# Three key tiles of 128 and a block diagonal rest tile in a fused attention and feed-forward kernel

## The chip, the cores and the metric

The kernel runs on one core of a Trainium2 chip. The metric is the device time of one execution in microseconds (us), the median of several runs; lower is better. Most runs of one kernel agree within about 1%. A profile of one execution comes with each kernel. Engines are named as the profile names them: PE (TensorE matmul), PEld (TensorE weight load), DVE (VectorE), ACT (ScalarE), POOL (GpSimd) and SP (SyncE, which issues most DMAs here; SPq is its queue).

## The reference, cut to what matters

There are 8 batches of 12 heads, 448 tokens and a head size of 64. The heads are worked in pairs, so there are 6 pairs per batch and 48 in all. After the attention comes a feed-forward layer of 768 by 2048 by 768.

```python
q_n = q / sqrt(mean(q*q, -1) + 1e-6) * g_q          # k_n likewise
scores = (1 / sqrt(64)) * q_n @ k_n.T
attn = softmax(scores)
x = (attn @ v)  -> [3584, 768]
h = x @ w_in
out = (h * clip(h + 3, 0, 6) / 6) @ w_out
```

Everything arrives in 32-bit floats; the kernel multiplies in bf16.

## The kernel before

The program is a list of steps. Each step names the engine or engines that may take it, an estimate of its time, and the steps that it must wait for. A greedy planner in the kernel's own source orders the steps of each engine once, before the program is built, so on the chip every engine runs a fixed order. "Batch 2's slot" is the stretch in which the attention of batch 2 runs; the feed-forward work of batch 1 runs in the same stretch.

Loads: three DMAs per pair, each of 112 partitions with four tokens of each head (1024 contiguous bytes).

```python
def heads(src, P):
    b, j = divmod(P, NJ)
    return src[b, 2*j:2*j+2, :, :].rearrange("h (p t) d -> p h (t d)", t=T)      # T = 4
def loads(P):
    for i, src in enumerate((k, q)):
        e = "ACT" if i and P < 3 else "SP"
        add(e, 0.47, at - 26, lambda: dma_start(out=qk[0:PT, i], in_=heads(src, P)), ...)   # PT = 112
    add("SP", 0.47, at - 19, lambda: nc.sync.dma_start(out=vf[0:PT], in_=heads(v, P)), ...)
```

Preparation: squares, their sums on VectorE, the norm factor on ScalarE, then one scaling of k and one of q, on VectorE or GpSimd (GpSimd alone from batch 2 on).

```python
red = add("DVE", 0.6 * n, ..., tensor_reduce(out=ssq, in_=sq ...))
r   = add("ACT", 0.45, ..., rstd, red)
sc.append(add({"DVE": 0.69, "POOL": 1.05}, 0, ..., tensor_tensor(qks, qk, rs4 (broadcast), MULT), r, lock=True))
```

Then come the transposes of k and q (on PE for the first ten pairs, by DMA after), four score steps of 112 keys per pair (two matmuls each, one per head, on the two halves of the PE's rows), one exp of 896 columns per step, and 64 value matmuls of 65 columns per two pairs.

## Time and profile before

The median is 442.9 us (441.35 to 443.99). The first table of the profile gives the busy time of each engine, its share of the span and the number of its instructions:

```profile
PE 410.6 (94%) x3663; PEld 229.2 (52%) x3682; DVE 246.3 (56%) x417; ACT 249.0 (57%) x425; POOL 240.2 (55%) x230
```

The windows table gives the busy time of each engine per stretch, with the number of instructions in brackets. After the engines come the granted TensorE clock (1.00 is full), the busy share of the core's DMA engines and the rate they moved, in GB/s. The kernel before:

```profile
core 0: us, PE busy (x) PEld busy (x) DVE busy (x) ACT busy (x) POOL busy (x), PEclk, DMA share, GB/s
0.00:10.00 10.00, 0.00 (x0) 0.00 (x0) 0.44 (x1) 2.39 (x4) 3.34 (x18) 1.00 0.88 241
10.00:20.00 10.00, 4.62 (x28) 1.89 (x29) 9.85 (x14) 7.01 (x17) 4.52 (x6) 1.00 1.12 249
20.00:30.00 10.00, 9.52 (x120) 6.23 (x121) 9.07 (x17) 8.59 (x13) 8.29 (x9) 1.00 1.15 266
30.00:40.00 10.00, 8.78 (x136) 5.63 (x132) 8.91 (x20) 8.73 (x15) 9.55 (x10) 1.00 1.18 254
40.00:90.00 50.00, 45.63 (x485) 26.34 (x486) 38.08 (x65) 35.49 (x65) 44.45 (x43) 1.00 1.06 209
90.00:140.00 50.00, 49.41 (x452) 26.06 (x453) 33.62 (x52) 32.80 (x56) 31.68 (x28) 1.00 0.63 163
```

PE is nearly full from 60 us on. In 10 to 40 us VectorE is 89 to 98% busy, GpSimd fills up too, and the DMA share is over 1. The chain of waits that ended last puts most of the span on PE:

```profile
PE 80%; POOL 5%; DVE 4%; ACT 3%; issue 3%; DMA 3%; SPq 1%; POOLq 0%
```

The timeline of SP in 20 to 31 us (start, duration in us, source line, what is loaded from what) shows how long the issue of one load holds the queue, here mostly 0.31 us:

```profile
24.08 0.31 SPq L302 DMA_DIRECT2D qk<-in_q_dram  x1
24.64 0.31 SPq L306 DMA_DIRECT2D vf<-in_v_dram  x1
27.90 0.31 SPq L302 DMA_DIRECT2D qk<-in_k_dram  x1
```

The list of DMA issues gives count, size and median time from issue to landing over the whole run:

```profile
qk<-in_k_dram SPq DMA_DIRECT2D x48, 224.0 KB, 3.3
vf<-in_v_dram SPq DMA_DIRECT2D x48, 224.0 KB, 3.7
```

### The profile page before, as it was taken

Reading aid. Unit: us, or ns where it says so; the run is one execution under the profiler, and the core shown is the slowest. Engines: PE = TensorE matmul, PEld = TensorE weight load, DVE = VectorE, ACT = ScalarE, POOL = GpSimd, SP = SyncE. Lnnn points to the kernel's source line nnn. Section 1 sums busy time; section 2 is a strip of 40 time slices with the busy share of each in tenths; the row PEclk is TensorE's granted clock in tenths of the full one; section 3 lists DMA queues with packets and bytes.
Section 4 is the critical chain, followed back from the end, with each engine's and each line's share of the span. In section 5 each row is a group of like instructions: output and inputs, shape, how many; then the busy total and the mean of one; then the engine's idle time right before and its main releaser. Section 6 shows DMA issues by size and latency. Waiting matters only on the chain.

```text
span 438.6 us, 9205 instructions
## 1 busy us (share of the span) xinstructions
PE 410.6 (94%) x3663; PEld 229.2 (52%) x3682; DVE 246.3 (56%) x417; ACT 249.0 (57%) x425; POOL 240.2 (55%) x230
## 2 busy tenths in 40 slices
PE   0588799999999999999999999999999999999995
PEld 0355455555455565554455565554455555654563
DVE  1998887657674564456555465556564444334421
ACT  3788588657765666367664677357673665123200
POOL 3499988855757567656765657747757510000000
PEclk9999999999999999999999999999999999999999
DMA  8999999877545745674465655684465420220122
GB/s 241 247 265 261 224 214 193 216 197 192 128 121 148 189 113 136 167 214 111 133 156 157 177 135 145 159 214 109 120 161 164 97 56 12 54 81 0 37 72 73
DMA packets 102923, 64.58 MB, mean 147 GB/s; under 512 B 59744, under 2 KB 99424, under 8 KB 102880
## 3 DMA queue, kind: packets, MB, share of 16 engines
q1 hardware_dynamic: 94544, 57.01, 50.6%
q0 software_dynamic: 7296, 6.29, 9.1%
q10 hardware_dynamic: 1040, 0.69, 0.5%
q8 instruction: 29, 0.48, 0.5%
q14 instruction: 14, 0.11, 0.1%
HBM read 45.61 MB, written 11.01 MB: 129 GB/s over the span
## 4 chain that ended last, share of the span: by engine, by line
PE 80%; POOL 5%; DVE 4%; ACT 3%; issue 3%; DMA 3%; SPq 1%; POOLq 0%
PE M L558 27%; PE M L533 25%; PE S L416 9%; PE X L437 8%; PE S L558 4%; PE R L437 2%; PE S L533 2%; DVE ssq L337 1%; ACT e L421 1%; POOL qks L351 1%; PE X L558 1%; POOL sq L322 1%; POOL va L359 1%; DMA gq_t<-in_g_q_dram 1%; POOL sq L329 1%
## 5 line engine op out<-in xcount | busy, mean ns | idle before, releaser
L421 ACT ACTIVATE e<-S 112x896 bf16<-112x896 f32 x192 | 166.3, 914 | 64.1 <-PE S L416 64.0
L533 PE MATMUL M<-xT,w_in_sb 128*128 128x384 bf16 (+1 forms) x679 | 145.1, 349 | 3.7 <-DVE gT L541 2.9
L351 POOL TENSOR_TENSOR qks<-qk,rs 112x512 bf16<-112x512 f32 x87 | 90.5, 1055 | 86.6 <-ACT rs L344 84.7
L558 PE MATMUL M<-w_out_sb,gT 128*128 128x384 bf16 x736 | 131.8, 326 | 0.0
L558 PEld LDWEIGHTS <-gT 128*128 128x128 bf16 x896 | 82.9, 98 | 57.8 <-issue 7.8
L533 PEld LDWEIGHTS <-w_in_sb 128*128 128x128 bf16 x768 | 69.6, 97 | 67.4 <-issue 12.5
L541 DVE SCALAR_TENSOR_TENSOR gT<-t,M 128x384 bf16<-128x384 f32 (+1 forms) x116 | 70.6, 611 | 59.1 <-ACT t L539 58.3
L539 ACT ACTIVATE t<-M 128x384 f32<-128x384 f32 (+1 forms) x116 | 62.6, 540 | 67.0 <-PE M L533 65.5
L437 PEld LDWEIGHTS <-e 112*128 112x128 bf16 x1536 | 65.1, 99 | 31.4 <-issue 16.0
L337 DVE TENSOR_REDUCE ssq<-sq 112x16 f32<-112x1024 f32 (+1 forms) x49 | 58.4, 1193 | 23.3 <-POOL sq L329 12.2
L329 POOL TENSOR_TENSOR sq<-qk 112x1024 f32<-112x1024 f32 x36 | 68.1, 1892 | 0.0
L416 PE MATMUL S<-kq,kp 64*128 64x448 bf16 x384 | 56.6, 364 | 4.1 <-DVE kp L381 1.7
L437 PE MATMUL X<-va,e 112*128 112x65 bf16 x1152 | 58.6, 196 | 0.8 <-ACT e L421 0.6
L566 DVE COPY y<-M 128x384 f32<-128x384 f32 x46 | 25.6, 556 | 59.2 <-PE M L558 59.0
L359 POOL CAST va<-vf 112x512 bf16<-112x512 f32 x48 | 31.5, 658 | 10.4 <-DMA vf<-in_v_dram 10.1
L392 POOL TENSOR_SCALAR kp<-kq,gp 128x448 bf16<-128x448 bf16 x23 | 32.3, 1402 | 5.3 <-DMA kq<-qks 5.2
L463 DVE TENSOR_TENSOR xn<-X,rd 128x384 bf16<-128x384 f32 x48 | 26.8, 558 | 1.6
L416 PEld LDWEIGHTS <-kp 64*128 64x128 bf16 x384 | 12.2, 94 | 27.7 <-issue 18.0
L437 PE MATMUL R<-va,e 112*128 112x65 bf16 x384 | 20.4, 195 | 0.0
L377 PE MATMUL M<-ident,qks 112*128 112x112 bf16 x80 | 7.9, 242 | 13.0 <-DVE qks L351 12.4
L558 PE MATMUL S<-w_out_sb,gT 128*128 128x384 bf16 x112 | 19.5, 326 | 0.0
L462 DVE RECIPROCAL rd<-X 128x6 f32<-128x6 f32 x48 | 9.2, 192 | 15.3 <-PE X L437 15.2
(42 smaller groups left out, 156.2 us busy)
## 6 DMA issues: line engine op xcount, KB each, us to landing
qk<-in_k_dram SPq DMA_DIRECT2D x48, 224.0 KB, 3.3
vf<-in_v_dram SPq DMA_DIRECT2D x48, 224.0 KB, 3.7
qk<-in_q_dram SPq DMA_DIRECT2D x45, 224.0 KB, 3.4
w_in_sb<-in_moe_w_in_dram POOLq DMA_DIRECT2D x4, 768.0 KB, 11.3
w_out_sb<-in_moe_w_out_dram POOLq DMA_DIRECT2D x4, 768.0 KB, 11.9
out_dram<-y SPq DMA_DIRECT2D x8, 336.0 KB, 3.1
out_dram<-y SPq DMA_DIRECT2D x8, 288.0 KB, 3.4
out_dram<-y SPq DMA_DIRECT2D x8, 240.0 KB, 3.2
```

Source lines behind the costliest of these rows:

```text
L329: parts = [add("POOL", 1.93, at - 10, lambda: nc.gpsimd.tensor_tensor(out=sq[0:PT], in0=qk[0:PT], in1=qk[0:PT], op=MULT), *ld, *war, lock= ...
L337: red = add("DVE", 0.6 * n, at - 8 * hurry + 0.5 * i0, lambda i0=i0, i1=i1, cs=cs: nc.vector.tensor_reduce(out=ssq[0:PT, cs], in_=sq[0:PT, ...
L351: sc.append(add(on, 0, at - 6 * hurry, lambda e, i=i, rs4=rs4: engines[e].tensor_tensor(out=qks[0:PT, i].rearrange("p t h d -> p h t d"), ...
L359: vc = add({"POOL": 0.61}, 0, at - 3, lambda e: engines[e].tensor_copy(out=va[0:PT, :, :, 0:D], in_=vf[0:PT].rearrange("p h (t d) -> p h t ...
L392: nc.vector if e == "DVE" else nc.gpsimd).tensor_scalar_mul(
L416: nc.tensor.matmul(out=ps[:, a, 0:S], lhsT=kp[rows, c0:c0 + 128], rhs=kq[rows, 1, :], start=True, stop=True)
L421: x = add("ACT", 0.93, at + step * (t0 + i) / T + 0.2, lambda t=t0 + i, ps=ps: nc.scalar.activation(out=e[0:PT, t], in_=ps[0:PT, :, 0:S], ...
L437: nc.tensor.matmul(out=dst[:, a * E1:(a + 1) * E1], lhsT=e[0:PT, t, a, c0:c0 + 128], rhs=va[0:PT, a, t, :], start=(first and a == 0 and t ...
L533: nc.tensor.matmul(out=m[:, 0:n], lhsT=w_in_sb[:, kt, f * 128:(f + 1) * 128], rhs=X[:, kt, :], start=(kt == 0), stop=(kt == NKT - 1))
L539: r = add("ACT", 0.08 + n / 1200, due + span, lambda: nc.scalar.activation(out=t[:, 0:n], in_=m[:, 0:n], func=RELU, bias=0.5, scale=1.0 / ...
L541: g = add("DVE", 0.12 + n / 960, due + span, lambda: nc.vector.scalar_tensor_tensor(out=G[:, f, :], in0=t[:, 0:n], scalar=1.0, in1=m[:, 0: ...
L558: nc.tensor.matmul(out=m[:, 0:HALF], lhsT=G[:, f, i * 128:(i + 1) * 128], rhs=w_out_sb[:, f, cols], start=(f == 0), stop=(f == NFT - 1))
```

## The change

The intent is to take work off PE. 448 keys are cut into three tiles of 128 and a rest of 64 instead of four tiles of 112. The rests of the two heads of a pair share one tile, laid out block diagonally: the rows of head 0 carry head 0's rest keys in columns 0 to 63, those of head 1 in columns 64 to 127. Two pairs then need seven score steps instead of eight, and 48 full value matmuls and 16 half-row ones instead of 64. The price is a load of k and of v in two DMAs each, and one more VectorE instruction per pair, which scales the rest keys and sets them on the diagonal by a mask. Besides, only 8 instead of 10 pairs are transposed on PE, no feed-forward output group of batch 0 stays in its own slot (two groups, 5.2 us of PE, move one slot later), and the small loads of g go to the front of ScalarE's queue, pair 0's q to SP's. From batch 1 on the pairs are worked two at a time, and the results of the value matmuls go to one PSUM tile (X) instead of two (X and R).

```diff
+    def load_tiled(e, at, tile_, src, P, war, cost, after):
+        x = heads(src, P)                                        # [2, 448, 64]
+        most = add(e, 0.47, at, lambda: engine.dma_start(
+            out=tile_[:, 0:2 * NS].rearrange("p (h t) d -> p h (t d)", h=2),
+            in_=x[:, 0:SM].rearrange("h (p t) d -> p h (t d)", t=NS)), ...)      # 128 rows, 768 bytes
+        rest = add(e, 0.47, at, lambda: engine.dma_start(
+            out=tile_[:, 2 * NS], in_=x[:, SM:S]), ...)          # [2, 64, 64]: 128 rows of 256 bytes
...
+        def scale_rest():
+            nc.vector.scalar_tensor_tensor(
+                out=qks[:, NS].rearrange("p (h d) -> p h d", h=2),
+                in0=kf[:, 2 * NS].unsqueeze(1).to_broadcast([128, 2, D]),
+                scalar=rs[:, 2 * NS:2 * NS + 1], in1=head[:], op0=MULT, op1=MULT)
+        sr = add("DVE", 0.26, at - 9 * hurry, scale_rest, r[0], head_make, *qwar, lock=True)
...
-    NPE = 10
+    NPE = 8
-    START, FIRST, PAIR = 9.0, 4.1, 2.3
+    START, FIRST, PAIR = 9.0, 3.7, 2.1
-    SPLIT = [2] + [0] * (B - 3) + [0, 0]
+    SPLIT = [0] + [0] * (B - 3) + [0, 0]
-    g_load = add("ACT", 2.2, 0, load_g, after=1.5, late=3.0)
+    g_load = add("ACT", 1.95, -99, load_g, after=0.7, late=1.0)
...                      # attend, gather: seven steps per two pairs, half-row rest-value matmuls
```

## The prediction

> **What bounds the kernel now.** The windows table shows the tensor engine (PE) busy 8.8 of 10 us in 30-40, 45.6 of 50 in 40-90, and 49.3 to 50.0 of each 50 us from 90 to 390. The chain of waits puts 80% of the span on PE.
>
> 1. *0 to 14 us.* ScalarE waits until 8.89 us (timeline, ACT: idle 6.89, DMA of g): the small g loads sit in its queue behind three q loads, each waiting for a DMA to land; pair 0's K was there at about 4.2. First PE instruction: 11.69.
> 2. *14 to about 60 us.* Attention of batch 0, start of batch 1. VectorE is 91 to 98% busy, ScalarE over 85%; PE waits for them. First exps of pairs 0, 6, 12: 14.9, 42.4, 83.5 us.
> 3. *60 to 438 us.* PE bound. Start to start (timeline): 128x384 matmul 162 ns, 128x512 216, 65-column value matmul 33, two-head score step 196. Entering a score cluster costs 258 instead of 162, leaving it 282 instead of 196: 0.18 us of mode switch per cluster. This agrees with the Trainium skill, "TensorEngine Tiling (Array Packing)", Key Properties: changing the tiling mode drains the engine, while tiles of one mode run in parallel (the two heads' matmuls start 4 ns apart here).
>
> **PE, per two pairs.** Before: 4 score clusters 4x0.18 + 8x0.196 = 2.29; 64 value matmuls x 0.033 = 2.11; sum 4.40. After (instruction order): 3 switched clusters 0.54; 6 two-head steps 1.18; two full-row rest steps about 0.38; 48 value matmuls 1.58; 16 half-row rest-value matmuls riding in the score clusters, 0.3 to 0.6 (estimate: 33 ns per overlapping pair, or per matmul). Sum 3.98 to 4.28: saves 0.12 to 0.42. Times 21 (batches 1 to 7): 2.5 to 9; I take 7 us. Two pairs fewer transposed on PE: 16x0.04 = 0.6 us.
>
> **ScalarE.** 192 exps of 914 ns become 165 full ones and 6 half ones (0.56 us, estimate from the Trainium skill, "ScalarE: Activation LUTs", What ACT_TABLE_LOAD costs: 186 ns + 0.833 per column; its 932 for 896 columns is near the trace's 914). This counts only in batch 0: 4x0.914+0.43 = 4.1 per pair now, about 3.75 then. VectorE's load per pair hardly moves (reduce 15/16, rest scaling +0.25), so I expect 1.3 us of the 2.1.
>
> **Start.** g goes first on ScalarE's queue, pair 0's q moves to SP: squares near 5 to 6 instead of 8.89; I take 3 us.
>
> **Moved.** The two y groups (5.2 us of PE) leave batch 1's slot for batch 2's: batch 1's slot shrinks from 41 to 34-36 us, then set by VectorE and GpSimd; batch 2's grows by 5. Net about 0.
>
> **Cost.** k and v loads split in two (96 more DMAs, 256-byte rows), two more DMA transposes. DMA share is 0.6 in the PE-bound part, so off the path; at the start (1.1) they may take back 1 us.
>
> **Sum.** 442.9 - 7 - 0.6 - 1.3 - 3 + 1, about 432. Predicted 431.5 us, 8 in 10: 426 to 437. Faster by over 2% (below 434.1): 0.70; within 2%: 0.28; slower: 0.02.
>
> **Right if:** first PE at 8 to 9.5 us; pair 6's first exp at 37 to 38.5; value plus rest matmuls of two pairs about 2.0 us; PE over 98% busy after 90; full exps 0.92 us. **Wrong if:** rest-value matmuls don't overlap or add drains; the single X buffer or the merged pairs make PE wait for VectorE or the exps; more DMAs in flight delay loads, so that GpSimd starves in batches 0 and 1; or VectorE sets batch 0 and nothing of ScalarE's gain shows.

## The result, and the profile after

The changed kernel takes 472.9 us (471.62 to 475.03), the kernel before 442.2 in the same job. The ratio is 1.069, with a 95% interval of 1.064 to 1.075. A ratio here is the mean time of one kernel's fast runs over the mean of the other's fast runs of the same rounds, so it is not quite the ratio of the medians that are quoted. Three runs of those told below counted as slow, one each of e11, e13 and e18 (over 1.5% above the fastest of their kernel); the ratios leave them out, and so do the medians quoted for these three. A gain from one experiment to another is best read from the ratios, since the jobs differ.

The same views as above, for the kernel after. Busy time by engine:

```profile
PE 408.0 (87%) x3601; PEld 231.8 (49%) x3618; DVE 262.4 (56%) x485; ACT 230.7 (49%) x404; POOL 225.9 (48%) x265
```

The windows, with the same stretches and columns:

```profile
0.00:10.00 10.00, 0.39 (x4) 0.34 (x4) 2.48 (x6) 3.57 (x8) 3.78 (x19) 1.00 0.58 161
10.00:20.00 10.00, 6.88 (x57) 3.49 (x55) 8.00 (x14) 7.18 (x13) 4.65 (x6) 1.00 0.92 178
20.00:30.00 10.00, 3.58 (x41) 2.19 (x38) 5.91 (x11) 3.74 (x9) 7.50 (x9) 0.68 0.98 202
30.00:40.00 10.00, 6.87 (x90) 4.24 (x85) 4.92 (x12) 6.44 (x10) 4.08 (x5) 0.81 0.81 175
40.00:90.00 50.00, 24.55 (x239) 14.59 (x239) 27.64 (x51) 16.64 (x34) 29.64 (x34) 0.75 0.93 181
90.00:140.00 50.00, 44.38 (x452) 24.53 (x452) 31.40 (x59) 31.92 (x57) 36.32 (x40) 0.95 0.82 165
```

PE is idle where it was busy: 3.58 of 10 us in 20 to 30 (before 9.52), 24.55 of 50 in 40 to 90 (before 45.63). But no other engine took over as the limit: VectorE, full before, is only half busy in 20 to 90 us, and ScalarE and GpSimd have gaps as well. In 0 to 40 us the DMA engines move less, 161 to 202 GB/s where they moved 241 to 266, and their busy share is lower (0.58 to 0.98; single stretches of 10 us after that reach 1.2). In these 40 us all engines wait, and what they wait for is slow without being full. The granted clock falls as well (0.68 to 0.81), in the stretches where PE idles.

The chain of waits, by engine and by line:

```profile
PE 61%; DMA 10%; DVE 8%; POOL 7%; SPq 7%; issue 5%; ACT 2%; POOLq 0%; DVEq 0%
PE M L683 22%; PE M L658 18%; DMA vf<-in_v_dram 6%; PE X L578 6%; PE S L493 5%; PE S L683 4%; POOL sq L352 3%; SPq L320 3%; DMA kf<-in_k_dram 3%; PE S L658 2%; DVE gT L666 2%; PE X L683 2%; SPq L334 1%; DVE qks L389 1%; SPq L323 1%
```

DMA and SP's queue, which issues the loads, had 4% of the span together and now have 17%. Three of the five longest waits of 0 to 140 us (engine and line, for what; total us, times, longest) show the same chain: GpSimd waits for k, VectorE for GpSimd, PE for VectorE.

```profile
PE M L658 <- DVE gT L666: 19.0, 8, 10.2
DVE ssq L368 <- POOL sq L352: 18.9, 7, 7.6
POOL sq L352 <- DMA kf<-in_k_dram: 17.4, 8, 5.7
```

The timeline of SP in 23 to 32 us:

```profile
23.96 0.60 SPq L320 DMA_DIRECT2D vf<-in_v_dram  x1
24.61 1.40 SPq L323 DMA_DIRECT2D vf<-in_v_dram  x1
26.13 3.63 SPq L320 DMA_DIRECT2D kf<-in_k_dram  x1
29.81 0.53 SPq L323 DMA_DIRECT2D kf<-in_k_dram  x1
30.45 1.56 SPq L334 DMA_DIRECT2D qf<-in_q_dram  x1
```

An issue that held the queue 0.31 us now holds it up to 3.63 here, and up to 4.93 in the run (before: 2.00). 31 issues of plain DMAs in the run take over 0.8 us (before: 5). All nine that take over 2.5 us come right behind a rest load; in 0 to 100 us the median load behind a rest load takes 1.08 us to issue, the median load behind another plain load 0.46 (rest loads themselves left out). SP's queue is issuing 85 to 94% of each 20 us in 0 to 100 us. Before, it was 23 to 38% in 0 to 60 us; from 60 to 100 us, with its DMA transposes, that queue too was at 84 to 90%, and PE was full all the same. The list of issues shows the two new kinds of load; the profile of this kernel gives no landing times:

```profile
kf<-in_k_dram SPq DMA_DIRECT2D x48, 192.0 KB
...
kf<-in_k_dram SPq DMA_DIRECT2D x48, 32.0 KB
```

The first exp of a batch marks where the batch starts. From the timelines, in us:

| kernel | batch 0 | batch 1 | batch 2 | batch 5 | end | batch 5 to end |
|---|---|---|---|---|---|---|
| before | 14.9 | 42.4 | 83.5 | 227.2 | 438.6 | 211.4 |
| after | 13.6 | 53.9 | 111.1 | 263.0 | 471.3 | 208.3 |

Of the 32.7 us between the two profiled spans, 27.6 are lost before batch 2 starts. Batches 2 to 4 take 8.2 more, 5.2 of which are the output groups that moved there. From batch 5 on the new kernel is 3.1 us faster.

### The profile page after: what moved, and what is told of

The parts are those of the page before. It is cut to its first block, busy times and chain, and to the rows that moved or that the text cites. A ratio compares the mean times of both kernels' runs of the same rounds, so it can differ in the third digit from the quotient of the medians.

```text
span 471.3 us, 9379 instructions
## 1 busy us (share of the span) xinstructions
PE 408.0 (87%) x3601; PEld 231.8 (49%) x3618; DVE 262.4 (56%) x485; ACT 230.7 (49%) x404; POOL 225.9 (48%) x265
## 4 chain that ended last, share of the span: by engine, by line
PE 61%; DMA 10%; DVE 8%; POOL 7%; SPq 7%; issue 5%; ACT 2%; POOLq 0%; DVEq 0%
PE M L683 22%; PE M L658 18%; DMA vf<-in_v_dram 6%; PE X L578 6%; PE S L493 5%; PE S L683 4%; POOL sq L352 3%; SPq L320 3%; DMA kf<-in_k_dram 3%; PE S L658 2%; DVE gT L666 2%; PE X L683 2%; SPq L334 1%; DVE qks L389 1%; SPq L323 1%
## 5 line engine op out<-in xcount | busy, mean ns | idle before, releaser
L526 ACT ACTIVATE e<-S 128x896 bf16<-128x896 f32 x144 | 125.1, 915 | 52.2 <-PE S L493 52.2
L683 PEld LDWEIGHTS <-gT 128*128 128x128 bf16 x896 | 83.4, 98 | 53.9 <-issue 2.5
L368 DVE TENSOR_REDUCE ssq<-sq 128x15 f32<-128x960 f32 (+2 forms) x49 | 55.2, 1128 | 32.1 <-POOL sq L352 23.5
L578 PEld LDWEIGHTS <-e 128*128 128x128 bf16 x1152 | 54.1, 100 | 22.5 <-issue 3.6
L411 POOL CAST va<-vf 128x448 bf16<-128x448 f32 x48 | 27.1, 565 | 77.3 <-PE X L578 35.8
L578 PE MATMUL X<-va,e 128*128 128x65 bf16 x1152 | 59.9, 197 | 0.0
L352 POOL TENSOR_TENSOR sq<-kf 128x448 f32<-128x448 f32 x44 | 41.8, 949 | 23.2 <-DMA kf<-in_k_dram 19.7
L382 POOL TENSOR_TENSOR qks<-kf,rs 128x384 bf16<-128x384 f32 x43 | 36.7, 854 | 30.4 <-ACT rs L375 17.7
L352 POOL TENSOR_TENSOR sq<-qf 112x512 f32<-112x512 f32 x44 | 46.0, 1045 | 3.1 <-DMA qf<-in_q_dram 2.9
L395 POOL TENSOR_TENSOR qks<-qf,rs 112x512 bf16<-112x512 f32 x42 | 44.6, 1061 | 0.0
L389 DVE SCALAR_TENSOR_TENSOR qks<-kf,rs,head 128x128 bf16<-128x128 f32 x48 | 27.0, 571 | 13.0 <-DMA kq<-qks 9.3
```

The source lines that it names most:

```text
L352: engines[e].tensor_tensor(out=o, in0=x, in1=x, op=MULT)
L368: lambda i0=i0, i1=i1, rows=rows: nc.vector.tensor_reduce(out=ssq[0:rows, i0:i1], in_=sq[0:rows, i0:i1], axis=AX_X, op=ADD),
L382: engines[e].tensor_tensor(out=qks[:, 0:NS].rearrange("p t (h d) -> p h t d", h=2), in0=kf[:, 0:2 * NS].rearrange("p (h t) d -> p h t d", ...
L389: nc.vector.scalar_tensor_tensor(out=qks[:, NS].rearrange("p (h d) -> p h d", h=2), in0=kf[:, 2 * NS].unsqueeze(1).to_broadcast([128, 2, D ...
L395: engines[e].tensor_tensor(out=qks[0:PT, 4:4 + T].rearrange("p t (h d) -> p h t d", h=2), in0=qf[0:PT].rearrange("p (h t) d -> p h t d", h=2),
L526: lambda dst=dst, ps=ps, w=2 if whole else 1: nc.scalar.activation(out=dst, in_=ps[:, 0:w, 0:S], func=EXP), s, *(AVW[P] if t < NS else AVR ...
```

## The experiments

The new rest load is a DMA whose outermost dimension is 2 (the heads). The Trainium skill, "DMA: Bandwidth & Descriptors", section "Why a DMA increments its semaphore by 16 and not by 1", says that the hardware takes the slowest dimension that is not 1 on each side and spreads the DMA over the largest number of engines, up to 16, that divides both (here 2 in DRAM and 128 in SBUF). "Rules for kernel authors" on the same page says it as a rule: an outermost dimension of size c under 16 confines the whole DMA to at most c engines. So each rest load would run on two engines, 64 rows each. The trace does not name a packet's engine, but it fits: worked out from the packets' starts and durations, at most 4 of the 256-byte packets are in flight at once in 0 to 60 us. Wide loads with packets of the same size (e2 below) have up to 12.

Theories, with the letters that the quoted texts use. N: the narrow shape of the rest loads is the loss. C: their number is. S: the two small moves of the change are (NPE and SPLIT). O: the planned order is too hurried for batch 0.

### e1_rest_by_head: rest loads wide, but twice as many

```diff
-        rest = add(e, 0.47, at, lambda: engine.dma_start(out=tile_[:, 2 * NS], in_=x[:, SM:S]), ...)
+        rest = [add(e, 0.47, at, lambda h=h: engine.dma_start(
+            out=tile_[h * 64:(h + 1) * 64, 2 * NS], in_=x[h, SM:S]), ...) for h in range(2)]
```

> The changed kernel; each 32 KB rest load of k and v (two heads x 64 keys x 256 bytes) is cut into two loads of one head, 64 rows each. Theory N (narrow load: [...]): cut by head the outermost dimension is 64, the load is spread, and the time falls from 472.9 to 428-438 us, with the first 90 us back to about 240 GB/s. Rival C (count: more DMAs per pair, eight in flight at most, each 0.5 us to issue): 7 loads per pair instead of 5 make it worse, 478 us or more. Rival S (schedule: PE transposes only to pair 7, y groups moved): no change, 470-475.

Measured: 478.8 us, ratio 1.083 (1.078 to 1.087). Up to 11 small packets are now in flight, and it is slower still, as C said. So N alone falls: seven wide loads per pair cost 6 us more than five of which two are narrow.

### e2_before_wide and e3_before_narrow: the loads alone, on the kernel before

An unread load of 32 KB is added beside each k and v load of the kernel before. In e2 its shape is 128 rows of 256 bytes; in e3 it is [2, 64, 64], as in the change.

```diff
+    def extra(src, P, due, cost, after):
+        junk, _, _ = junk_r.take()
+        add("SP", 0.47, due, lambda: nc.sync.dma_start(out=junk[:], in_=src[b, 2*j, 0:128]), ...)              # e2
+        add("SP", 0.47, due, lambda: nc.sync.dma_start(out=junk[:], in_=src[b, 2*j:2*j+2, SM:S]), ...)         # e3
```

> The kernel before, with one more load per pair and per k and v, to a tile that nobody reads: 128 rows of 256 bytes, outermost dimension 128. Five loads per pair as in the changed kernel, same bytes and packets as its rest loads. Theory N: 442-447 us[...]. Rival C: the number of DMAs is what costs, 460 us or more.

> As e2_before_wide, but the unread load has the changed kernel's shape: two heads x 64 rows, outermost dimension 2; same number of DMAs, packets and bytes as e2. Theory N: 455-480 us, and its 256-byte packets are at most 2 to 4 in flight where those of e2 are near 10. Rival C: the same as e2_before_wide within 1%.

Measured: e2 453.7 us, ratio 1.027 (1.022 to 1.031); e3 476.2 us, ratio 1.077 (1.070 to 1.083). The kernel before of that job took 441.5. So 96 more wide loads cost 12 us, and their narrow shape 22 more. Together that is as much as the whole change lost, on a kernel that has nothing else of the change. Both N and C are half right. The windows of 10 to 50 us tell the two apart; e2, then e3:

```profile
10.00:50.00 40.00, 26.27 (x277) 15.48 (x278) 29.51 (x49) 24.17 (x41) 25.26 (x28) 0.87 1.12 243
```

```profile
10.00:50.00 40.00, 21.86 (x226) 12.67 (x227) 25.31 (x43) 23.51 (x42) 22.78 (x25) 0.84 0.89 187
```

In e3 the rate falls to 187 GB/s as in the changed kernel (which has 182 there), and VectorE to 25.31 of 40 us (25.42 there); in e2 the rate stays at 243. SP's queue is issuing 94% of 10 to 60 us in e3 and 42% in e2. The timeline of SP in e3 has the same long issues, at the loads that follow a narrow one:

```profile
25.74 0.53 SPq L300 DMA_DIRECT2D junk<-in_v_dram  x1
26.31 2.63 SPq L316 DMA_DIRECT2D vf<-in_v_dram  x1
29.04 0.62 SPq L300 DMA_DIRECT2D junk<-in_k_dram  x1
29.70 3.46 SPq L311 DMA_DIRECT2D qk<-in_k_dram  x1
```

### e6_before_tiny: few bytes, same number

As e2, with 16 rows (4 KB) per unread load.

```diff
-        ... out=junk[:],    in_=src[b, 2 * j, 0:128]
+        ... out=junk[0:16], in_=src[b, 2 * j, 0:16]
```

> As e2_before_wide (453.7 us), but the unread loads move 16 rows of 256 bytes instead of 128: the same number of DMAs, an eighth of the packets. If the 12 us of e2 come from the number of DMAs (issue time on the SP queue, eight outstanding): 450-455 us. If they come from small packets taking the DMA engines' time: 442-446 us.

Measured: 452.1 us, ratio 1.022 (1.019 to 1.025), within 2 us of e2. What e2 pays is the number of DMAs, not their bytes or packets.

### e4_after_two_undone: the two small moves

```diff
-    NPE = 8
+    NPE = 10
-    SPLIT = [0] + ...
+    SPLIT = [2] + ...
```

> The changed kernel with two of its parts undone: PE transposes up to pair 9 again, two y groups of batch 0 again in batch 1's slot. Rival S: 440-455 us. Theories N and C: 466-476 us, no verdict at 2%.

Measured: 468.4 us, ratio 1.059 (1.055 to 1.063). That is 4 to 5 us of the loss. S is rejected as the main cause.

### e5_rest_by_batch: few and wide rest loads

The rests of a whole batch come in two DMAs for k and two for v, with 64 partitions outermost. A batch has 22 loads (changed kernel 30, before 18). GpSimd's squares and casts of the rest become instructions of their own.

```diff
+            x = src[b, :, SM:S, :].rearrange("(j a) p d -> a p j d", a=2)
+            ... [engine.dma_start(out=t[a * 64:(a + 1) * 64], in_=x[a]) for a in range(2)]    # once per batch
```

> The changed kernel with the rest keys and values of a whole batch loaded at once: two DMAs for k and two for v per batch (64 rows x 6 pieces of 256 bytes, outermost dimension 64), so 22 loads per batch instead of 30, none narrow; GpSimd and the squares work on the rest in an extra 64-column instruction. Everything else of the change stays. Theory L (the loads' shape and number cost what the change lost; its savings on PE are there): 428-438 us, SP queue issuing below 50% of the time in 0-60 us (now about 90%), first exp of pair 6 at 38-42 us (now 53.9). If some other part of the change costs (merged pairs, single X buffer, schedule): still above 450.

Measured: 459.2 us, ratio 1.036 (1.031 to 1.040). 14 us of the loss are gone, but not all of it. The window of 10 to 50 us:

```profile
10.00:50.00 40.00, 24.47 (x236) 13.99 (x236) 33.88 (x56) 22.07 (x41) 26.38 (x42) 0.76 1.14 244
```

The rate is back at 244 GB/s and VectorE is busy again (33.88 of 40; the kernel before has 37.14 there), yet PE has 24.47 where the kernel before has 30.18. The markers of the expectation were missed: SP's queue is still issuing 64% of 0 to 60 us, and pair 6's first exp came at 56.5 us. Something else holds as well.

### e7_after_late_weights, e8_batch_late_weights, e9_batch_slow_plan, e10_batch_g_pool: four guesses at the remainder

e7 and e8 start the weight loads 13 us later, in the changed kernel and in e5. e9 is e5 planned at 4.6 us per pair of batch 0. e10 is e5 with g loaded from GpSimd's queue.

```diff
-    GATE, W_IN_AT, W_OUT_AT, W_STEP = 2, 7.0, 35.0, 6.3          # e7, e8
+    GATE, W_IN_AT, W_OUT_AT, W_STEP = 2, 20.0, 48.0, 6.3
-    START, FIRST, PAIR = 9.0, 3.7, 2.1                           # e9
+    START, FIRST, PAIR = 9.0, 4.6, 2.1
-            nc.scalar.dma_start(out=gq_t[...], ...)              # e10, and gk_t
+            nc.gpsimd.dma_start(out=gq_t[...], ...)
```

> The changed kernel with the eight weight loads planned 13 us later (first at 20 instead of 7, w_out from 48). Theory B (in the first 60 us the DMA queues are the bound: weights and loads compete, a load takes 6 to 9 us to land and the eight outstanding loads are not enough): with no weights in the first 20 us loads land in about 3 us and pair 5's first exp comes at 40 us or earlier (49.1 in the changed kernel); total 455-468 us since the weights' work only moves. Rival O (the static order of the merged pairs is what stalls, whatever the DMAs do): pair 5 at 47-51 us.

> e5_rest_by_batch with the weights 13 us later. Theory B: first exp of pair 6 at 40-46 us (56.5 in e5), total 440-450. Rival O: 455-460.

> e5_rest_by_batch with the plan's pace of batch 0 set from 3.7 to 4.6 us per pair, so that loads and preparation of later pairs stand less far ahead of attention in the in-order queues. Rival O (the plan is too fast for the loads, so late data block work that could run): 440-450 us. Theory B alone: 455-462 us.

> e5_rest_by_batch with the four small g loads issued by GpSimd instead of ScalarE, so that they take none of the eight outstanding places of the hardware queues in the first 6 us. Theory B: the first 10 us move over 210 GB/s (187 in e5, 241 before) and the total falls by 2 to 6 us. Rival O: no change within 1%.

Measured: e7 469.6 (1.064; 1.058 to 1.070), e8 457.1 (1.035; 1.028 to 1.042), e9 458.5 (1.038; 1.035 to 1.041), e10 462.1 (1.047; 1.042 to 1.051). These are two runs each. By the ratios each is within 5 us of the kernel it was made from. Neither the weights, nor the planned pace (O), nor g is the remainder. But the late weights did what B said to batch 0: in e7 pair 5's first exp came at 39.5 us instead of 49.1. Batch 1 then took 59.8 us instead of 57.2, and the total hardly moved. In e8 batch 2 starts at 95.3 us (e5: 105.6), and batches 2 to 4 take 7 us longer. So a gain in an early batch need not reach the end. In e8 VectorE is 92 to 99% busy in each 10 us of 10 to 50, which pointed at VectorE.

### e11_after_no_loads and e12_before_no_loads: no loads at all from pair 5 on

Their outputs are wrong, which doesn't matter for the times. The steps stay in the plan, so the order of all other instructions is untouched; only the DMAs are left out, and the buffers keep the data of pairs 0 to 4. The loads of these first five pairs are still there, in each kernel's own form. Theory L: the loads are the whole loss. Rival D: a good part is the work on VectorE and GpSimd.

```diff
-        most = add(e, 0.47, at, lambda: engine.dma_start(
+        most = add(e, 0.47, at, lambda: None if P >= 5 else engine.dma_start(        # likewise rest, q, v
```

> Wrong result on purpose: the changed kernel with the loads of k, q and v left out from pair 5 on (the buffers keep the data of pairs 0 to 4), the order of every other instruction untouched. Theory L, the loads (their number and the narrow rest loads) are the whole loss, and the savings on the tensor engine are there as predicted: this kernel is 7 to 13 us faster than e12, the same edit on the kernel before; pair 6's first exp at about 38 to 44 us (pairs 0 to 4 still have their loads), batch 1 under 40 us. Rival D, a good part of the loss is the changed kernel's order of work on VectorE and GpSimd in batches 0 and 1, whatever the loads do: this kernel is no faster than e12 or up to 15 us slower, and batches 0 and 1 are still 10 us or more longer than in e12, with VectorE over 90% busy there.

> Wrong result on purpose: the kernel before with the loads left out from pair 5 on. What the loads cost there at all. Both theories: 435 to 442 us, batch 0 and 1 shorter by a few us (DMA share falls from 1.1 to under 0.8 in 20 to 90 us), the part after 90 us unchanged, since the tensor engine sets it.

Measured: e11 454.1 us without its slow run (455.7 with it, which later expectations quote; ratio 1.027; 1.021 to 1.034), e12 441.7 us (0.997; 0.993 to 1.002). By the ratios, which here span two jobs, the loads left out cost the kernel before 1 us and the changed one 18: 17 us of the loss are these loads. The other 13 remain without them. L falls as the whole cause, and what D expected came. How much of the 13 is still loads is open: up to 30 us e11 runs as the changed kernel does, on the loads of pairs 0 to 4 (PE 3.30 of 10 us in 20 to 30, where the changed kernel has 3.58 and e12 10.00). So the 17 us need not be all that the loads cost. Windows of the first 47 us of batch 1, e11 and then e12:

```profile
51.00:98.00 47.00, 34.85 (x366) 20.47 (x368) 42.39 (x64) 27.64 (x53) 36.17 (x41) 0.96 0.81 120
```

```profile
43.00:90.00 47.00, 42.72 (x447) 24.39 (x444) 35.16 (x61) 32.38 (x59) 41.34 (x40) 0.96 0.76 107
```

Now VectorE is the limit, 42.39 of 47 us, and it has 7 us more work than in e12. Its costliest new group there and, for comparison, one of its other groups, in 0 to 98.3 us of e11 (count | busy us, mean ns | idle before it):

```profile
L389 DVE SCALAR_TENSOR_TENSOR qks<-kf,rs,head 128x128 bf16<-128x128 f32 x16 | 17.0, 1069 | 0.9 <-ACT rs L375 0.7
L666 DVE SCALAR_TENSOR_TENSOR gT<-t,M 128x384 bf16<-128x384 f32 x16 | 8.4, 550 | 1.8 <-ACT t L664 1.7
```

The new instruction, on 128 elements per partition, takes 1069 ns on average; the gT instruction, of the same kind and on 384 elements, takes 540 to 555 each time. The shortest run of the new one is 335 ns, the longest 3.09 us. In all of e11, the 10 of its 48 runs that no GpSimd instruction overlaps take 335 to 352 ns, and the other 38 take 339 to 3093; 14 of the 16 gT above are overlapped too. The timeline shows what the longest one meets, VectorE and then GpSimd:

```profile
76.85 0.55 DVE L666 SCALAR_TENSOR_TENSOR gT<-t,M 128x384 bf16<-128x384 f32 x1 [0.22 <-ACT t L664]
77.32 3.09 DVE L389 SCALAR_TENSOR_TENSOR qks<-kf,rs,head 128x128 bf16<-128x128 f32 x1
```

```profile
77.39 1.03 POOL L352 TENSOR_TENSOR sq<-qf 112x512 f32<-112x512 f32 x1
78.39 0.82 POOL L382 TENSOR_TENSOR qks<-kf,rs 128x384 bf16<-128x384 f32 x1
79.17 1.03 POOL L395 TENSOR_TENSOR qks<-qf,rs 112x512 bf16<-112x512 f32 x1
80.16 0.66 POOL L411 CAST va<-vf 128x448 bf16<-128x448 f32 x1
```

VectorE's instruction begins at 77.32 and ends at 80.41. GpSimd runs three multiplications back to back from 77.39 to 80.20 meanwhile. The new instruction reads two operands from SBUF (the rest keys and the mask); gT reads one from SBUF and one from PSUM. The Trainium skill, "SBUF — State Buffer", section "Who interferes with whom", says that a VectorE instruction with two SBUF inputs contends with a GpSimd instruction that reads SBUF, and that the port pair they share is an exclusive lock. The trace agrees, and it shows more than one GpSimd instruction passing before VectorE gets its turn (the times on GpSimd are rough, but 3.09 us is longer than any of those instructions). No run changed the operands alone, so the reason is read from the trace and the page and not tested.

### e13_two_pairs_per_load and e14_two_pairs_act_squares: fewer loads still, and work moved to ScalarE

e13 is e5 with k, q and v of two pairs in one DMA, 13 loads per batch, fewer than the kernel before has. e14 also lets ScalarE take squares in batches 0 and 1.

```diff
+            x = src[b, 2 * j:2 * j + 2 * m, 0:n, :]               # m = 2 pairs, from pair 2 on
+            ... dma_start(out=tile_[0:rows, s:s + m]..., in_=x.rearrange("h (p t) d -> p h (t d)", t=t))
-                {"DVE": 0.68 * c, "POOL": 1.04 * c} if P < 2 * NJ ...                              # e14
+                {"ACT": 0.63 * c, "DVE": 0.68 * c, "POOL": 1.04 * c} if P < 2 * NJ ...
```

> The version with the rests of a batch in four wide loads (e5_rest_by_batch, 459.2), and from pair 2 on k, q and v of two pairs in one load: 13 loads per batch instead of 22 (before: 18, after: 30). Theory L: fewer loads than the kernel before has, so most of the loss is recovered: 430 to 445 us. Rival D: the loads were no longer the limit in e5, so 452 to 460 us, VectorE over 90% busy in 20 to 70 us as in e5. A third possibility: loads twice as large land later and make batch 0 wait more, over 460 us.

> The same, with the squares of batches 0 and 1 allowed on ScalarE too, which was only 40 to 60% busy in 20 to 70 us of e5. Rival D: VectorE and GpSimd get some 10 us of work less in batches 0 and 1, so 5 to 12 us faster than e13. Theory L: within 3 us of e13.

Measured: e13 456.1 us without its slow run (1.032; 1.026 to 1.038), e14 454.5 us (1.028; 1.023 to 1.034). Nine loads per batch fewer are worth 2 us, so at least the number of loads had ceased to be the limit in e5. e14 is 1.5 us faster than e13 by the ratios, within the noise. VectorE and GpSimd did lose 13.6 us of squares in 0 to 100 us, but the 5 to 12 us that D expected of it did not come.

### e15_no_loads_act_rest and e16_after_act_rest: the new instruction taken off VectorE

In batches 0 and 1 two half-row ScalarE instructions do the scaling of the rest keys; the zeros off the diagonal are set once at the start. e15 does it to e11 (wrong result), e16 to the changed kernel. Theory V: this instruction is what is left of the loss. Rival W: the wait moves to the next instruction on VectorE.

```diff
+        def scale_rest_act():
+            for a in range(2):
+                h = slice(a * 64, a * 64 + 64)
+                nc.scalar.activation(out=qks[h, NS, h], in_=kf[h, 2 * NS], func=COPY, scale=rs[h, 2 * NS:2 * NS + 1])
+        if P < 2 * NJ:
+            sr = add("ACT", 0.5, at - 6.5 * hurry, scale_rest_act, r[0], qks_make, *qwar)
```

> Wrong result on purpose: e11 (the changed kernel without loads from pair 5 on, 455.7) with one more edit: in batches 0 and 1 the scaling of the rest keys goes from one VectorE instruction to two half-row ones on ScalarE. In e11 those 16 instructions took 17.1 us on VectorE, up to 3.09 us each, where the shortest took 0.335: the prediction had 0.25. Theory V, this instruction, held up beside GpSimd's work, is what is left of the loss once the loads are gone: VectorE has 17 us less to do, and this kernel is 8 to 16 us faster than e11, 440 to 448, about e12 (441.7) or below. Rival W, VectorE and GpSimd hold each other up whatever the instruction is, so that the wait only moves to the next one on VectorE: within 4 us of e11.

> The changed kernel with its loads as they are and the same edit alone (the rest keys of batches 0 and 1 scaled on ScalarE). There the 16 instructions took 9.6 us in all. If the loads hide it: 467 to 473, less than 6 us faster than the changed kernel (472.9). If V is the larger of the two causes by itself: under 463.

Measured: e15 445.8 us (1.008; 1.004 to 1.013), e16 469.3 us (1.062; 1.056 to 1.068). In e15 the edit is worth 8 us, the lower edge of what V expected, and W is rejected. In e16 the same edit is worth 3 to 4: with the loads in place, an instruction that is slow on VectorE costs little. The same 47 us in e15, to set beside those of e11:

```profile
51.00:98.00 47.00, 41.81 (x437) 24.67 (x434) 39.82 (x60) 33.33 (x63) 45.60 (x48) 0.93 0.76 113
```

PE has 41.81 us there instead of 34.85, and batch 1 takes 37.4 us instead of 46.6. The edit has a cost of its own: the plan now puts pair 3's squares on VectorE ahead of pair 0's last copy, VectorE waits there for a load until 14.61 us, and the first exp comes at 18.3 instead of 12.9 us. That wait is longer than the 4 us by which e15 is still behind e12, but whether it is what is left was not tested: e15 had made the delay up by batch 1, which starts at 51.1 us there and at 51.7 in e11.

### e17_act_rest_two_pairs and e18_old_then_new: two tries at a version that beats both

e17 is e14 with the rest scaling on ScalarE, and the next batch's rest loads issued 7 to 9 us later.

```diff
-        kr, kr_use, krl = load_rest("SP", at - 26, kr_r, k, P, max(0.7, at - 24))
+        kr, kr_use, krl = load_rest("SP", at - 17, kr_r, k, P, max(0.7, at - 17))      # v: at - 19 -> at - 12
```

> The candidate: e14 (454.5: rests by batch, two pairs per load, squares of batches 0 and 1 allowed on ScalarE) with the rest keys of batches 0 and 1 scaled on ScalarE (16 instructions, 13.5 us on VectorE in e14), and the rest loads of the next batch issued 7 to 9 us later. Theory V: 441 to 448, level with the kernel before or a little slower or faster. Rival W: 451 to 456.

Measured: 464.4 us (1.049; 1.042 to 1.056), slower than e14. My second edit spoiled it: the later rest loads meet the first DMA transpose on SP's queue. The timeline of SP, and the windows row of 58 to 70 us, in which PE runs for 0.97 us and VectorE not at all:

```profile
46.48 6.26 SPq L328 DMA_DIRECT2D kr<-in_k_dram  x2
52.92 7.82 SPq L481 DMA_TRANSPOSE kq<-qks  x1
```

```profile
58.00:70.00 12.00, 0.97 (x26) 0.84 (x24) 0.00 (x0) 1.42 (x3) 4.80 (x9) 0.62 1.31 178
```

The transpose begins its issue at 52.92 us, takes 7.82 us over it and lands at 70.3. This run says nothing about V, since two things were changed at once.

e18 keeps batches 0 and 1 as in the kernel before (apart from more memsets on GpSimd at the start the same instructions in the same order, up to the point where work for batch 2 begins), and uses the new tiles from batch 2 on, with the rest loads of e5.

```diff
+        for fn, fo, at in ((loads, loads_o, -26), (prep, prep_o, -13), (turn, turn_o, -2)):
+            blocks.append((use_at[P] + at, lambda fn=fo if P < P0 else fn, P=P: fn(P)))    # P0 = 12
+        if P < P0:
+            blocks.append((begin[P], lambda P=P: attend_o(P)))
+            blocks.append((begin[P + 1] + 0.1, lambda P=P: gather_o(P)))
```

> The version meant to beat both: batches 0 and 1 as in the kernel before (same instructions in the same order), the three key tiles, the block diagonal rest tile and the seven steps per two pairs from batch 2 on, where the tensor engine sets the pace, with the rest loads of a batch in two wide loads for k and two for v; the y split of batch 0 as before. From what the runs showed after batch 2's first exp (before 355.1 us; e5 352.9 and e11 354.1, each with 5.2 us of y work more): 5 to 7 us less than before. If the explanation holds, batch 2 starts at 83 to 85 us as before and the time is 434 to 439 us, ratio 0.98 to 0.993. If the new layout costs the later batches something that the earlier traces hid, or if the saving on the tensor engine is not there: 440 or more.

Measured: 450.3 us without its slow run, ratio 1.020 (1.016 to 1.024). The expectation of 434 to 439 missed. Batch 0 is as before (27.4 us), but batch 1 takes 47.5 instead of 41.1, batches 2 to 4 take 5.4 more, and only from batch 5 on is it faster, by 2.8. PE's busy time did fall:

```profile
PE 406.4 (91%) x3630; PEld 230.2 (51%) x3646; DVE 269.5 (60%) x470; ACT 235.5 (53%) x407; POOL 241.9 (54%) x341
```

It is 4.2 us less than before; but PE waits more, in 140 to 240 us for a VectorE that is late:

```profile
PE M L940 <- DVE gT L948: 4.1, 5, 2.1
```

VectorE has 23 us more work over the run than before (269.5 against 246.3); the new instruction alone takes 25.9, and in that stretch it waits 8.9 us in its own queue for squares on GpSimd. Why batch 1 lost 6 us was not tested: the loads, transposes and squares for batch 2 fall into it, but nothing tells their shares apart. No version here beats the kernel before.

The batch starts of these kernels, in us, to read beside the table above:

| kernel | batch 0 | batch 1 | batch 2 | batch 5 | end | batch 5 to end |
|---|---|---|---|---|---|---|
| e5 | 13.6 | 56.5 | 105.6 | 249.7 | 458.5 | 208.8 |
| e11, no loads, after | 12.9 | 51.7 | 98.3 | 243.9 | 452.4 | 208.5 |
| e12, no loads, before | 15.4 | 43.5 | 86.3 | 229.3 | 440.8 | 211.5 |
| e15, e11 with rest on ScalarE | 18.3 | 51.1 | 88.6 | 235.8 | 443.8 | 208.0 |
| e18 | 15.8 | 43.2 | 90.7 | 239.8 | 448.4 | 208.6 |

## Why the prediction was wrong

It gave 431.5 us and got 472.9. Two of its terms were mis-sized, and what that cost lies mostly in the first two batches. With both taken away 27 of the 41 us are gone (472.9 to 445.8, e15); the rest is told under what stays open.

- **The step that failed first is "Cost".** It read: "k and v loads split in two (96 more DMAs, 256-byte rows) ... DMA share is 0.6 in the PE-bound part, so off the path; at the start (1.1) they may take back 1 us." The mechanism was named, in "Wrong if" ("more DMAs in flight delay loads, so that GpSimd starves in batches 0 and 1"), but sized at 1 us. It measured 17 us, the loads of pairs 0 to 4 not counted (e11 and e12 against the kernels with loads); added to the kernel before alone it measured 34 (e3), 12 of them for the number (e2) and 22 for the narrow shape. The share of the DMA engines was the wrong thing to read. The narrow loads did not fill the engines (share 0.89 in e3, 1.12 in e2, in 10 to 50 us); they lengthened the issue of the load behind them on SP's queue, and with it the wait of what came after, in a stretch where VectorE was already 89 to 98% busy.
- **The second is "VectorE's load per pair hardly moves (reduce 15/16, rest scaling +0.25)".** The new instruction takes 0.335 us when nothing disturbs it, close to the guess, but 1.07 on average beside GpSimd in batches 0 and 1 of e11. Taking it off VectorE there was worth 8 us (e15). With the loads in place most of it was hidden: 3 to 4 us (e16). The before profile had the warning: the scaling instructions on VectorE, also with two SBUF operands, took 0.89 us on average in 0 to 56 us where their shortest took 0.68, and the squares took up to 2.55.
- **PE's saving was right.** Predicted: 7 us for 21 pairs of pairs and 0.6 for the transposes. PE's busy time of e11 and e12 differs by 8.3 us, as the first table of each shows, e11 and then e12:

```profile
PE 404.0 (89%) x3601; PEld 231.3 (51%) x3618; DVE 279.3 (62%) x485; ACT 231.0 (51%) x404; POOL 225.9 (50%) x265
```

```profile
PE 412.3 (94%) x3663; PEld 229.9 (52%) x3682; DVE 245.6 (56%) x417; ACT 249.0 (56%) x425; POOL 240.4 (55%) x230
```

In the changed kernel only 2.6 of it shows in the busy time, at a mean clock of 0.956. PE was over 98% busy, as predicted for all that follows 90 us, only from 290 us on: 89% in 90 to 140, 97% in 140 to 290. From batch 5 on, where PE sets the pace, the changed kernel gains 3.1 us, which is what 7 us give for three of seven batches. The half-row rest-value matmuls run in overlapping pairs, 4 ns apart, as the prediction's reading of "TensorEngine Tiling (Array Packing)" said.
- **The start was nearly right** in its first half: the first PE instruction came at 9.61 us (predicted 8 to 9.5, before 11.69), but the first exp gained 1.3 us only, of 3.
- **Pair 6's first exp** was predicted for 37 to 38.5 us and came at 53.9. That marker failed at once and put the loss where it is.
- **ScalarE's exps were right**: 0.915 us for a full one, 0.53 for a half one (predicted 0.92, and 0.56 as an estimate from the Trainium skill, "ScalarE: Activation LUTs", "What ACT_TABLE_LOAD costs"). Since batch 0 waited for other things, nothing of it showed.
- **"Moved ... net about 0"** can't be read in the changed kernel, whose batch 1 took 57.2 us. In e15, without the loads and the new instruction there, batch 1 took 37.4 (predicted 34 to 36).

What stays open: e15 at 445.8 us is still 15 above the prediction's sum without its 1 us for loads (430.5). 13 of these 15 are lost before batch 1, which starts at 51.1 us where 37 to 38.5 was predicted: in the stretch that still has the loads of pairs 0 to 4. What they, the late start and the order of the plan each cost there was not separated. The single X tile and the pairs worked two at a time, which the prediction named as dangers, were not tested apart; from batch 5 on, where both are in use, the kernel gains. e5's remaining distance to the kernel before was taken apart only by the kernels without loads. With loads, e17 was to show it and failed for another reason. e18's loss in batch 1 is unexplained. How much of the wait is the length of an issue and how much the late landing behind it was not separated either: e1 has no issue over 2 us on SP's queue and was the slowest of all. There is a rival for what the number costs. In the traces of before, e1, e2 and e5 never more than eight DMAs of SP and ScalarE lie between issue and landing, and a small load takes one of these places as a large one does. No run changed that number.

## What to carry to other kernels

When a change splits a load, look at the outermost dimension of each new DMA and at the time that its issue holds the queue, not only at bytes and at the share of busy DMA engines; 96 small loads off the critical path on paper cost 12 us when wide and 34 when narrow. When a change adds a VectorE instruction where GpSimd is busy, cost it with the longest times that similar instructions with two SBUF operands have in that stretch, not with their shortest. And find the stretch with the least slack first: a saving of 7 us on the engine that holds 80% of the chain was lost four times over, most of it in the first quarter of the run, where other engines held it.

## What the Trainium skill lacked or had wrong

- "DMA: Bandwidth & Descriptors" says what confines a DMA to two engines, but no page says what such a DMA does to the queue that issues it: here the issues of loads behind a narrow one took up to 4.93 us, 1.08 in the median, instead of mostly 0.31, and SP's queue was issuing 94% of 10 to 60 us instead of 27%.
- The same page gives no price, in the time of a whole kernel, for more DMAs on one queue: 96 loads of 4 KB cost 10 us and 96 of 32 KB cost 12 in a kernel of 442 us (e6, e2).
- "SBUF — State Buffer", "Who interferes with whom", has the contention right. The same page ("SBUF: two separate sides") says that whichever starts first gets the port pair for the whole instruction and the other blocks; it does not say how often the loser can be passed over. In e11 one VectorE instruction that takes 0.335 us alone took 3.09 us beside three GpSimd instructions in a row, so the wait is not bounded by one instruction.
